# Stores moved to ScalarE's queue, a normalization tied behind the last gate, and norm sums placed between two parts of a product

## The chip, the cores and the metric

The kernel runs on one core of a Trainium2 chip. Five engines work side by side there, each with its own stream of instructions that it takes in order: TensorE (PE, matrix products, with PEld for its weight loads), VectorE (DVE), ScalarE (ACT), GpSimd (POOL) and SyncE (SP), which here only issues DMAs. They wait for one another by semaphores. TensorE writes to PSUM; VectorE and ScalarE read it from there. The metric is the time of one execution on the device, in microseconds.

## What is computed

Three layers follow one another, for a batch of B = 8 sequences of S = 576 tokens, with 8 heads of 64 and so 512 channels:

```python
kv = einsum('bhsd,bhse->bhde', k, v); out = einsum('bhsd,bhde->bhse', q, kv)
x = out / sqrt(mean(out*out, -1) + 1e-6) * g_norm          # per head and token; heads side by side: 512 channels
gate = sigmoid(sum_k conv_w[k] * x shifted by 4-k tokens)   # 5 taps, causal
x = (gate * (x @ w_val)) @ w_out
theta = x @ w_theta
y = w_tok_r @ (x * cos(theta)) + w_tok_i @ (x * sin(theta)) # over tokens
u = x + y;  result = u + relu(u @ w_ch)
```

Activations are 32-bit floats. The weights arrive as 64-bit floats and are decoded on the chip. Each large product is made of three: an operand is split into a rounded part (`h`) and the rest (`l`), and h·h, l·h and h·l are added up.

## The kernel before, in words

Channels lie on the 128 partitions, in four chunks (`m` or `k` = 0 to 3), and tokens along the free dimension, in two halves of 288.

**The first stage** is a loop over the batch, `for i in range(B)` at L392; below, "step i" is one pass of it. A step works on three batch elements at once:

- `value(i)` (L278): for each of four chunks `m`, 24 matmuls make `v` in a PSUM tile of two banks (L274 to L276 in `product`). VectorE multiplies it with the gate (L288, this is what "the gate" means below), ScalarE rounds it to `gh` (L68 in `parts`) and VectorE makes the rest `gl` (L69).
- `first(i)` (L294): the product with w_out, `y`, of four parts; each part runs over four chunks of `gh` and `gl`. Parts 0 and 1 first take chunks 0 to 2 and then chunk 3, since that chunk is finished last. ScalarE copies each finished part to `yo` (L304), two buffers, and SP's queue stores it to DRAM (L305).
- `conv(i + 1)` (L261): for each chunk one ScalarE instruction (L263), four of VectorE in a chain (L265), and the sigmoid (L266). Chunks 0 and 1 are traced at the end of step i, chunks 2 and 3 inside `value(i + 1)`.
- `normalize(i + 1)` (L237): from step 1 on VectorE multiplies `x` with the broadcast reciprocal roots `yb` (L246, two halves), then come `xh` on ScalarE (L68) and `xl` on VectorE (L69). In step 0 the factors come from TensorE instead (L254, L257).
- `attention(i + 2)` (L187), a generator in three pieces: two halves of `o` on TensorE (L200), whose squares (L204) and scaled copies (L205) ScalarE takes out of PSUM; then the norm sums, 64 small matmuls (L212) into one PSUM tile, and the chain of roots on VectorE (L219 to L225). The roots go to DRAM (`rd`, L228) and come back broadcast (`yb`, L233), both by SP's queue.
- `key_value(i + 2)` (L171) on TensorE (L182), and the loads of `kv` and `q` for step i + 3, by SP's queue (L156, L157, L168).

PSUM for all of this is one pool of four tiles of two banks. Each `v`, `y` and `o` tile, the key-value tile and the sums take one of the four and hold it until its reader is done.

**The decoded weights.** `w_theta` (4 pieces, the list `todo`) and the token weights (11 pieces, the list `toks`) are loaded raw (L85), decoded by VectorE and ScalarE (L94 to L98), and the decoded token pieces (`dst_tk`, two buffers) are stored to DRAM (L440) until the second stage loads them. They are traced at a low priority (`LATER`), so that they fill holes, and on VectorE behind the last normalizing instruction of the step (`issue_after(last.ins)`).

**The second stage** (from L444) has the phases, the mix over tokens and the last product; it follows the loop, and its first loads are traced in step 7.

**The order of work.** Python traces the instructions in program order, and a planner puts them into one order per engine: it takes the earliest traced of those that are ready by its own estimate of time, hands out buffers, and adds the semaphores. `issue_after(ins)` is an edge that puts what a block traces on the engine of `ins` behind `ins` in that engine's order; for other engines it says nothing. On the chip the order of each engine stands as planned, also where the real times are others.

Of the kernel before, what the change touches and what calls it, by code (L numbers as in the profile page):

```python
# [34 lines left out]
RATE = (1, 3)  # L35
# [8 lines left out]
def attention_moe_holo_kernel(ctx, tc, kvm, kvt, qt, gn, w_val, conv_w, w_out, w_th, w_tok, w_ch, outT):  # L44
# [5 lines left out]
    nc = tc.nc  # L50
# [8 lines left out]
    def two_banks(name):  # L59

        return pd.tile([P, 2, 512], F32, tag="pd", name=name)[:, :, :HS]
# [4 lines left out]
    def parts(h, l, src):  # L66

        one = nc.scalar.activation(h, src, AF.Copy)  # L68
        return nc.vector.tensor_tensor(l, src, h.bitcast(F32), ALU.subtract), one  # L69
# [18 lines left out]
    def decode(pool, raw, width, name, tag=""):  # L88

        if raw.dtype == F32:  # L90
            return raw
        dst = pool.tile([P, width if tag else DM], F32, tag="dst" + tag if pool is px else "fTt", bufs=(1 if tag else 2) if pool is px else 1, name=f"dst_{name}")[:, :width]
        lo, hi, d = raw[:, :width, 0], raw[:, :width, 1], dst.bitcast(I32)
        nc.vector.tensor_scalar(d, hi, 0x07FFFFFF, 3, ALU.bitwise_and, ALU.logical_shift_left)  # L94
        nc.vector.scalar_tensor_tensor(d, hi, -0x40000000, d, ALU.bitwise_and, ALU.bitwise_or)
        nc.vector.scalar_tensor_tensor(d, lo, 29, d, ALU.logical_shift_right, ALU.bitwise_or)
        nc.scalar.activation(hi.bitcast(F32), hi.bitcast(F32), AF.Square)
        nc.vector.scalar_tensor_tensor(dst, hi.bitcast(F32), TINY, dst, ALU.is_ge, ALU.mult)  # L98
        return dst
# [24 lines left out]
    ydram = [dr.tile([P, NM, S], F32, tag=f"yd{b}", name=f"yd{b}") for b in range(B)]  # L124
# [3 lines left out]
    tokdram = dr.tile([P, 9 * S], F32, tag="td", name="td")  # L128
# [3 lines left out]
    px = px_stack.enter_context(tc.tile_pool(name="px", bufs=1, reuse_waits="tile", side="right"))  # L132
# [104 lines left out]
    def normalize(b, x, y):  # L237


        xh = pa.tile([P, NM, S], F32R, tag="xh", bufs=1, name=f"xh{b}")  # L240
        xl = pa.tile([P, NM, S], F32R, tag="xl", bufs=1, name=f"xl{b}")
        for h in range(2):
            sl = slice(h * HS, (h + 1) * HS)
            v = x[:, :, PAD + h * HS:PAD + (h + 1) * HS]
            if b >= SPREAD:
                last = nc.vector.tensor_tensor(v, v, y[:, :, sl], ALU.mult)  # L246
            else:
                for g in range(2):
                    yb = two_banks(f"yb{b}_{h}_{g}")
                    for t in range(HS // TB):  # L250
                        for j in range(2):
                            k = 2 * g + j
                            rows = slice(32 * k, 32 * (k + 1))
                            nc.tensor.matmul(yb[:, j, t * TB:(t + 1) * TB], sel[rows, h * HS // TB + t, :], y[rows, :],  # L254
                                             start=True, stop=True, tile_position=(32 * k, 0))
                    ch = slice(2 * g, 2 * g + 2)
                    last = nc.vector.tensor_tensor(v[:, ch], yb, v[:, ch], ALU.mult)  # L257
            parts(xh[:, :, sl], xl[:, :, sl], v)
            yield (x, xh, xl), last

    def conv(b, m, x):  # L261
        a = pa.tile([P, S], F32, tag="acc", bufs=4, name=f"acc{b}_{m}")
        nc.scalar.activation(a, x[:, m, 0:S], AF.Copy, scale=cw[:, m * 5:m * 5 + 1])  # L263
        for k in range(1, 5):
            nc.vector.scalar_tensor_tensor(a, x[:, m, k:k + S], cw[:, m * 5 + k:m * 5 + k + 1], a, ALU.mult, ALU.add)  # L265
        nc.scalar.activation(a, a, AF.Sigmoid)  # L266
        return a

    def product(ps, w, m, xh, xl, t0, chunks=range(4)):
        tsl = slice(t0, t0 + HS)  # L270
        wh, wl = w
        for k in chunks:
            ks = slice(k * P, (k + 1) * P)
            nc.tensor.matmul(ps, wh[:, m, ks], xh[:, k, tsl], start=(k == 0), stop=False)  # L274
            nc.tensor.matmul(ps, wl[:, m, ks], xh[:, k, tsl], start=False, stop=False)  # L275
            nc.tensor.matmul(ps, wh[:, m, ks], xl[:, k, tsl], start=False, stop=(k == 3))  # L276

    def value(b, x, xh, xl, sg, between):  # L278
        gh = pa.tile([P, NM, S], F32R, tag="gh", bufs=1, name=f"gh{b}")
        gl = pa.tile([P, NM, S], F32R, tag="gl", bufs=1, name=f"gl{b}")  # L280
        for m in range(NM):
            between(m)
            g = sg[m]
            ps = two_banks(f"v{b}_{m}")
            for h in range(2):
                product(ps[:, h], wv, m, xh, xl, h * HS)
            halves = lambda t: t.rearrange("p (h s) -> p h s", h=2)
            nc.vector.tensor_tensor(halves(g), ps, halves(g), ALU.mult)  # L288
            parts(gh[:, m, :], gl[:, m, :], g)
            if m + EARLY < NM:  # L290
                sg.append(conv(b, m + EARLY, x))
        return gh, gl

    def first(b, gh, gl, between):  # L294
        y = [None] * NM

        def part(m, chunks):
            if y[m] is None:
                y[m] = two_banks(f"y{b}_{m}")
            for h in range(2):  # L300
                product(y[m][:, h], wo, m, gh, gl, h * HS, chunks)
            if 3 in chunks:
                yo = pa.tile([P, S], F32, tag="yo", bufs=2, name=f"yo{b}_{m}")
                nc.scalar.activation(yo.rearrange("p (h s) -> p h s", h=2), y[m], AF.Copy)  # L304
                nc.sync.dma_start(out=ydram[b][:, m, :], in_=yo)  # L305


        part(0, range(3))
        part(1, range(3))
        part(0, (3,))  # L310
        part(1, (3,))
        between()
        part(2, range(4))
        part(3, range(4))

# [46 lines left out]
    raw = {}  # L362
# [29 lines left out]
    for i in range(B):  # L392
        if i == B - 1:
            px_stack.close()
            qx = ctx.enter_context(tc.tile_pool(name="qx", bufs=1, reuse_waits="tile", side="right"))
            ys = load_y(0)
            tls = load_tails(0)
            for k in range(CHFIRST):
                weight_chunk(qx, wch, w_ch, k, "wc")
        two = i + 2 < B  # L400
        if two:
            ahead = attention(i + 2, qs.pop(i + 2))

        def between(m):

            if two and m == 1:
                key_value(i + 2, kvs.pop(i + 2))
                if i + 3 < B:
                    kvs[i + 3] = load_kv(i + 3)
            if two and m == 3:  # L410
                next(ahead)

        gs = value(i, *xs, sg, between)
        if two:
            next(ahead)
            if i + 3 < B:
                qs[i + 3] = load_q(i + 3)
        if i + 1 < B:
            *_, (nxs, last) = normalize(i + 1, *xy)
        if i == 0:  # L420
            for k in range(4):
                weight_chunk(px, wo, w_out, k, "wo", raw=raw[f"o{k}"])
        got = []
        first(i, *gs, lambda: got.append(next(ahead) if two else None))
        xy = got[-1]
        if i + 1 < B:
            xs = nxs
            sg = [conv(i + 1, m, xs[0]) for m in range(EARLY)]
        if 1 <= i < B - 1:
            with tc.high_priority(offset=-LATER), tc.issue_after(last.ins):  # L430
                for _ in range(RATE[0] if i < 6 else 8):
                    if todo:
                        w, src, k, name, scale = todo.pop(0)
                        weight_chunk(px, w, src, k, name, scale)
                for _ in range(RATE[1] if i < 6 else 11):
                    if toks:
                        j = toks.pop(0)
                        sl = slice(j * DM, min((j + 1) * DM, 9 * S))
                        raw = fetch(px, w_tok[:, sl], sl.stop - sl.start, f"tk_{j}")
                        nc.sync.dma_start(out=tokdram[:, sl], in_=decode(px, raw, sl.stop - sl.start, f"tk_{j}"))  # L440

# [7 lines left out]
    last = [None, None]  # L451
# [77 lines left out]
    def halves(b, then=None):  # L529

        nonlocal tls, zt
        f, *y = ys[b]
        if b % 2 == 0:
            zt = phase_tails(b, *tls)
            if then:
                then(8)
        return f, [zt[b % 2]] + phase(b, *y, then)
# [17 lines left out]
    for b in range(B):  # L555
        f, zs = nxt
# [53 lines left out]
```

## Time and profile before

| | us |
|---|---|
| median of 3 runs (lowest, highest) | 753.28 (752.94, 756.45) |
| the profiled execution | 753.31 |
| its span, first to last instruction | 751.5 |
| TensorE busy in the span | 709.7 (94%) |
| VectorE busy | 523.9 (70%) |
| ScalarE busy | 335.9 (45%) |
| mean granted TensorE clock | 0.986 |

Rows of the profile name the engine, the line of the kernel, the operation, and output <- input by the program's names; in a row of the timeline the first two numbers are the start and the length in us, and brackets at the end say how long the engine stood idle before it and what ended that. SPq is SP's DMA queue. Matmuls overlap, so their starts, 0.13 us apart at this size, say more than their lengths.

### The profile page before, as it was taken

Reading aid. Unit: us, or ns where it says so; the run is one execution under the profiler, and the core shown is the slowest. Engines: PE = TensorE matmul, PEld = TensorE weight load, DVE = VectorE, ACT = ScalarE, POOL = GpSimd, SP = SyncE. Lnnn points to the kernel's source line nnn. Section 1 sums busy time; section 2 is a strip of 40 time slices with the busy share of each in tenths; the row PEclk is TensorE's granted clock in tenths of the full one; section 3 lists DMA queues with packets and bytes.
Section 4 is the critical chain, followed back from the end, with each engine's and each line's share of the span. In section 5 each row is a group of like instructions: output and inputs, shape, how many; then the busy total and the mean of one; then the engine's idle time right before and its main releaser. Section 6 shows DMA issues by size and latency. Waiting matters only on the chain.

```text
span 751.5 us, 14674 instructions
## 1 busy us (share of the span) xinstructions
PE 709.7 (94%) x6000; PEld 669.9 (89%) x6000; DVE 523.9 (70%) x930; ACT 335.9 (45%) x560; POOL 20.7 (3%) x72
## 2 busy tenths in 40 slices
PE   1679999999989999889999999999999999999998
PEld 1568999798987999879899899999999998998998
DVE  6389969798879999588983872853853835836504
ACT  2366565637464645376541640621622514514301
POOL 4000000000000000000000000000000000000000
PEclk9779999999999999999999999999999999999999
DMA  9948794979896358534345034163051270160101
GB/s 256 285 140 243 209 229 141 229 228 237 219 238 189 108 136 246 190 102 122 111 138 157 9 119 113 32 174 90 17 164 59 69 179 35 64 175 1 64 1 64
DMA packets 77059, 104.88 MB, mean 140 GB/s; under 512 B 11712, under 2 KB 42560, under 8 KB 76992
## 3 DMA queue, kind: packets, MB, share of 16 engines
q1 hardware_dynamic: 76416, 101.85, 48.5%
q0 software_dynamic: 576, 2.10, 0.9%
q8 instruction: 47, 0.77, 0.4%
q14 instruction: 20, 0.16, 0.1%
HBM read 72.73 MB, written 31.19 MB: 138 GB/s over the span
## 4 chain that ended last, share of the span: by engine, by line
PE 60%; DVE 24%; DMA 8%; ACT 4%; issue 3%; SPq 1%; POOL 0%; DVEq 0%; ACTq 0%; POOLq 0%
PE u L513 10%; PE u L511 10%; PE u L512 10%; DVE acc L265 10%; PE c L276 5%; PE c L274 5%; PE c L275 5%; DMA yb<-rd 4%; PE th L459 3%; PE th L457 3%; PE th L458 3%; DMA kv<-in_kvm_dram 2%; DVE x L246 2%; DVE xl L69 2%; DVE acc L288 2%
## 5 line engine op out<-in xcount | busy, mean ns | idle before, releaser
L516 DVE TENSOR_TENSOR f<-u,f 128x288 f32<-128x288 f32 x64 | 26.5, 455 | 129.8 <-PE u L513 129.8
L265 DVE SCALAR_TENSOR_TENSOR acc<-x,cw,acc 128x576 f32<-128x576 f32 x128 | 100.8, 817 | 1.3 <-ACT acc L263 1.3
L68 ACT ACTIVATE uh<-f 128x288 fp32r<-128x288 f32 x64 | 26.2, 444 | 152.4 <-DVE f L516 152.3
L274 PE MATMUL y<-gh,woh 128*128 128x288 f32 x256 | 77.8, 304 | 7.8 <-DVE acc L288 5.4
L274 PE MATMUL v<-xh,wvh 128*128 128x288 f32 x256 | 77.6, 303 | 0.7 <-DVE acc L288 0.7
L276 PE MATMUL v<-xl,wvh 128*128 128x288 f32 x256 | 76.5, 299 | 0.0
L276 PE MATMUL y<-gl,woh 128*128 128x288 f32 x256 | 75.8, 298 | 0.5 <-DVE gl L69 0.5
L275 PE MATMUL y<-gh,wol 128*128 128x288 f32 x256 | 76.0, 297 | 0.0
L275 PE MATMUL v<-xh,wvl 128*128 128x288 f32 x256 | 76.0, 297 | 0.0
L274 PE MATMUL c<-uh,wch 128*128 128x288 f32 x256 | 75.4, 295 | 0.0
L276 PE MATMUL c<-ul,wch 128*128 128x288 f32 x256 | 75.4, 295 | 0.0
L275 PE MATMUL c<-uh,wcl 128*128 128x288 f32 x256 | 75.4, 294 | 0.0
L274 PEld LDWEIGHTS y<-gh,woh 128*128 128x128 f32 x256 | 48.8, 191 | 11.9 <-DVE acc L288 6.1
L274 PEld LDWEIGHTS v<-xh,wvh 128*128 128x128 f32 x256 | 48.7, 190 | 4.6 <-issue 1.7
L459 PE MATMUL th<-wth,yl 128*128 128x512 f32 x128 | 50.3, 393 | 0.0
L458 PE MATMUL th<-wtl,yh 128*128 128x512 f32 x128 | 50.1, 391 | 0.0
L457 PE MATMUL th<-wth,yh 128*128 128x512 f32 x128 | 50.0, 391 | 0.0
L276 PEld LDWEIGHTS y<-gl,woh 128*128 128x128 f32 x256 | 48.4, 190 | 1.2 <-DVE gl L69 1.2
L276 PEld LDWEIGHTS v<-xl,wvh 128*128 128x128 f32 x256 | 48.6, 190 | 0.3 <-issue 0.2
L275 PEld LDWEIGHTS y<-gh,wol 128*128 128x128 f32 x256 | 48.8, 191 | 0.0
L275 PEld LDWEIGHTS v<-xh,wvl 128*128 128x128 f32 x256 | 48.7, 190 | 0.0
L275 PEld LDWEIGHTS c<-uh,wcl 128*128 128x128 f32 x256 | 48.0, 188 | 0.3
(188 smaller groups left out, 1946.0 us busy)
## 6 DMA issues: line engine op xcount, KB each, us to landing
kv<-in_kvm_dram SPq DMA_DIRECT2D x32, 512.0 KB, 8.6
q<-in_qt_dram SPq DMA_DIRECT2D x32, 288.0 KB, 8.9
yd<-yo SPq DMA_DIRECT2D x32, 288.0 KB, 2.4
f<-yd SPq DMA_DIRECT2D x32, 288.0 KB, 3.7
out_dram<-f SPq DMA_DIRECT2D x64, 144.0 KB, 1.8
sd<-fT SPq DMA_DIRECT2D x64, 128.0 KB, 2.5
yt<-sd SPq DMA_DIRECT2D x8, 1024.0 KB, 5.6
yb<-rd SPq DMA_DIRECT2D x12, 576.0 KB, 8.0
```

What stands on the lines that cost most here:

```text
L68: one = nc.scalar.activation(h, src, AF.Copy)
L265: nc.vector.scalar_tensor_tensor(a, x[:, m, k:k + S], cw[:, m * 5 + k:m * 5 + k + 1], a, ALU.mult, ALU.add)
L274: nc.tensor.matmul(ps, wh[:, m, ks], xh[:, k, tsl], start=(k == 0), stop=False)
L275: nc.tensor.matmul(ps, wl[:, m, ks], xh[:, k, tsl], start=False, stop=False)
L276: nc.tensor.matmul(ps, wh[:, m, ks], xl[:, k, tsl], start=False, stop=(k == 3))
L457: nc.tensor.matmul(ps, yh[:, k, :], wth[0][:, k, :], start=(k == 0), stop=False)
L458: nc.tensor.matmul(ps, yh[:, k, :], wth[1][:, k, :], start=False, stop=False)
L459: nc.tensor.matmul(ps, yl[:, k, :], wth[0][:, k, :], start=False, stop=(k == 3))
L511: nc.tensor.matmul(ps[:, :HS], zh[:, ms], wkh[:, j, sl], start=(i == 0), stop=False)
L512: nc.tensor.matmul(ps[:, :HS], zh[:, ms], wkl[:, j, sl], start=False, stop=False)
L513: nc.tensor.matmul(ps[:, :HS], zl[:, ms], wkh[:, j, sl], start=False, stop=(i == 8))
L516: nc.vector.tensor_tensor(f[:, m, sl], ps[:, :HS], f[:, m, sl], ALU.add)
```

## The change

The diff has five parts:

1. `value` also returns the last `gl` instruction of VectorE, and the loop traces `normalize(i + 1)` under `issue_after` of it: all VectorE instructions of the normalization come behind the last gate's split in VectorE's order. Its ScalarE and TensorE instructions get no edge of their own.
2. The store of each `yo` is issued from ScalarE's queue instead of SP's (32 DMAs of 288 KB).
3. The store of each decoded token piece is issued from ScalarE's queue as well (11 DMAs).
4. In `first` the piece `between()`, which holds the norm sums, the roots and the DMAs of `rd` and `yb`, is traced after chunks 0 to 2 of parts 0 and 1, and no longer after their chunk 3.
5. The special rates for step 6 (8 weight pieces, 11 token pieces) go; the rates are 1 and 3 in every step.

```diff
@@ value
-            parts(gh[:, m, :], gl[:, m, :], g)
+            last, _ = parts(gh[:, m, :], gl[:, m, :], g)
...
-        return gh, gl
+        return gh, gl, last
@@ first
-                nc.sync.dma_start(out=ydram[b][:, m, :], in_=yo)
+                nc.scalar.dma_start(out=ydram[b][:, m, :], in_=yo)
...
         part(0, range(3))
         part(1, range(3))
+        between()
         part(0, (3,))
         part(1, (3,))
-        between()
         part(2, range(4))
         part(3, range(4))
@@ the loop
-            *_, (nxs, last) = normalize(i + 1, *xy)
+            with tc.issue_after(gs[2].ins):
+                *_, (nxs, last) = normalize(i + 1, *xy)
...
-        first(i, *gs, lambda: got.append(next(ahead) if two else None))
+        first(i, *gs[:2], lambda: got.append(next(ahead) if two else None))
...
-                for _ in range(RATE[0] if i < 6 else 8):
+                for _ in range(RATE[0]):
...
-                for _ in range(RATE[1] if i < 6 else 11):
+                for _ in range(RATE[1]):
...
-                        nc.sync.dma_start(out=tokdram[:, sl], in_=decode(px, raw, sl.stop - sl.start, f"tk_{j}"))
+                        nc.scalar.dma_start(out=tokdram[:, sl], in_=decode(px, raw, sl.stop - sl.start, f"tk_{j}"))
```

## The prediction

> **What bounds the kernel now.** I read the page's busy shares first, then TensorE's gaps in order of time, then what VectorE, ScalarE and the DMA queue did in each gap. The page, its first line and its shares:
>
> ```profile
> span 751.5 us, 14674 instructions
> ...
> PE 709.7 (94%) x6000; PEld 669.9 (89%) x6000; DVE 523.9 (70%) x930; ACT 335.9 (45%) x560; POOL 20.7 (3%) x72
> ```
>
> TensorE is busy 94%. The stretches below are steps 1 to 7 of the loop (from the first matmul of `v` to the next step's), the passage to the second stage, and that stage. Columns: stretch and its length, then busy us (instructions) of PE, PEld, DVE, ACT, POOL; granted clock; DMA share; GB/s.
>
> ```profile
> 89.56:121.65 32.09, 32.09 (x370) 30.04 (x369) 25.95 (x44) 18.18 (x28) 1.18 (x5) 1.00 0.73 187
> 121.65:155.88 34.23, 32.71 (x371) 30.12 (x369) 29.61 (x51) 19.48 (x30) 1.19 (x5) 1.00 0.85 220
> 155.88:189.06 33.18, 32.40 (x371) 29.95 (x369) 29.96 (x51) 19.40 (x31) 1.80 (x5) 1.00 0.84 224
> 189.06:224.19 35.13, 32.42 (x371) 30.07 (x370) 27.73 (x49) 17.99 (x29) 1.45 (x5) 1.00 0.89 223
> 224.19:258.91 34.72, 32.71 (x371) 29.97 (x370) 34.37 (x61) 21.39 (x34) 0.39 (x1) 1.00 0.52 159
> 258.91:286.11 27.20, 25.96 (x194) 25.49 (x193) 25.66 (x44) 14.17 (x23) 0.00 (x0) 1.00 0.51 146
> 286.11:315.26 29.15, 27.23 (x194) 27.00 (x193) 22.47 (x33) 10.74 (x17) 1.22 (x2) 0.94 0.68 211
> 315.26:334.00 18.74, 16.30 (x78) 13.14 (x76) 13.83 (x22) 12.32 (x19) 0.00 (x0) 1.00 0.44 130
> 334.00:751.50 417.50, 414.38 (x2853) 398.80 (x2853) 247.67 (x463) 157.10 (x282) 1.06 (x2) 1.00 0.30 89
> ```
>
> Step 1 has no gap in PE: 32.1 us is what a full step costs. Steps 2 to 5 do the same matmuls and take 2.1, 1.1, 3.0 and 2.6 us more (8.9 in all). Steps 6 and 7 have no attention ahead and no norm sums; there DVE (25.66 of 27.20) is nearly full too. From 334 us on the code is not touched, and PE is full. So the change can win at most those 8.9 us and a few of steps 6 and 7.
>
> TensorE's rows beside its gaps (start, length, [idle before <- what ended it]):
>
> ```profile
> 139.91 0.40 PE L274 MATMUL y<-gh,woh 128*128 128x288 f32 x1 [0.25 <-ACT x L205]
> ...
> 142.27 0.29 PE L276 MATMUL y<-gl,woh 128*128 128x288 f32 x1
> 143.55 0.41 PE L274 MATMUL y<-gh,woh 128*128 128x288 f32 x1 [0.99 <-DVE acc L288]
> ...
> 146.76 0.40 PE L276 MATMUL y<-gl,woh 128*128 128x288 f32 x1 [0.28 <-DVE gl L69]
> ...
> 205.65 0.29 PE L276 MATMUL v<-xl,wvh 128*128 128x288 f32 x1
> ...
> 207.27 0.40 PE L274 MATMUL y<-gh,woh 128*128 128x288 f32 x1 [0.20 <-ACT x L205]
> ...
> 209.62 0.29 PE L276 MATMUL y<-gl,woh 128*128 128x288 f32 x1
> ...
> 212.43 0.40 PE L274 MATMUL y<-gh,woh 128*128 128x288 f32 x1 [2.51 <-DVE acc L288]
> ...
> 243.34 0.71 PE L200 MATMUL o<-q,kvs 64*64 64x288 f32 x8 [0.85 <-ACT x L205]
> ...
> 273.57 0.40 PE L274 MATMUL y<-gh,woh 128*128 128x288 f32 x1 [0.98 <-ACT gh L68]
> ...
> 302.51 0.40 PE L274 MATMUL y<-gh,woh 128*128 128x288 f32 x1 [1.92 <-DVE acc L288]
> ```
>
> And VectorE there (steps 2, 4 and 6):
>
> ```profile
> 140.20 2.63 DVE L246 TENSOR_TENSOR x<-x,yb 128x1152 f32<-128x1152 f32 x2 [1.89 <-DMA yb<-rd]
> ...
> 204.91 0.76 DVE L69 TENSOR_TENSOR gl<-acc,gh 128x576 fp32r<-128x576 f32 x1 [0.81 <-ACT gh L68]
> 209.07 2.63 DVE L246 TENSOR_TENSOR x<-x,yb 128x1152 f32<-128x1152 f32 x2 [3.40 <-DMA yb<-rd]
> 211.62 0.75 DVE L288 TENSOR_TENSOR acc<-v,acc 128x576 f32<-128x576 f32 x1
> ...
> 216.58 1.36 DVE L69 TENSOR_TENSOR xl<-x,xh 128x1152 fp32r<-128x1152 f32 x1 [2.27 <-ACT xh L68]
> 217.85 1.54 DVE L265 SCALAR_TENSOR_TENSOR acc<-x,cw,acc 128x576 f32<-128x576 f32 x2
> ...
> 273.25 0.19 DVE L94 TENSOR_SCALAR dst_tk<-raw_tk 128x64 int32<-128x64 int32 x1
> ```
>
> This is the main finding. In step 4 the last matmul of `v` starts at 205.65, so its gate (L288) could run at about 205.95. But VectorE's order has the normalization (L246) ahead of it, and that stands 3.40 us for the broadcast `yb`, starts at 209.07 and takes 2.63 us: the gate runs at 211.62. TensorE meanwhile finishes the first three chunks of `y` part 0 (18 matmuls, to 209.62) and cannot begin part 1: the gate still holds the PSUM tile of the fourth `v`, one of the four in the pool. It goes on at 212.43. Step 2 is the same with 1.89 us of standing.
>
> **The change, part by part.**
>
> *Normalization behind the last gate (VectorE).* The gate then starts when `v` ends, 205.95, and ends at 206.7; part 1 wants its PSUM tile at 209.75. Cover: 3 us. The split that follows (gh 0.69, gl 0.76 and hand-overs) ends about 208.2, the fourth chunk wants it after 212. So three gaps go. By starts, less the usual 0.13 us between matmuls: 143.55 − 142.27 − 0.13 = 1.15; 212.43 − 209.62 − 0.13 = 2.68; and 0.28 at 146.76 as its row has it. Sum: **4.1 us**.
>
> The stall does not vanish, it moves to where it can stand: L246 now waits with `xl` and the convolutions (L265) behind it. In step 4 it starts at 209.07 as before, since the DMA sets it, and nothing but `xl` stands between it and L265: 209.07 + 2.63 + twice 1.3 for `xl` gives a convolution start near 214.3 to 215, against 217.85. In step 2: gl ends about 141.3 instead of L246 starting at 140.20, so L246 is 1.1 us later, and `gl` and gate no longer follow it (1.4 us): even. In steps 1, 3 and 5 the gate stood behind L246 without a gap in PE; there the same exchange wins nothing. Cost: 0, bounds −1 to +1.4 a step, hidden by PE's `y` phase of about 17 us until the next first gate.
>
> *Norm sums between the parts.* The same 64 matmuls, 12 matmuls earlier (1.6 us). Nothing is added on PE. They need all four squares (L204), and one PSUM tile that ScalarE must have emptied. ScalarE in steps 2 and 4:
>
> ```profile
> 145.66 0.65 ACT L204 ACTIVATE sq<-o 128x576 f32<-128x576 f32 x1
> ...
> 206.47 0.75 ACT L205 ACTIVATE x<-o,gsb 128x576 f32<-128x576 f32 x1
> 210.53 1.16 ACT L68 ACTIVATE xh<-x 128x1152 fp32r<-128x1152 f32 x1 [3.31 <-DVE x L246]
> 212.46 0.69 ACT L68 ACTIVATE gh<-acc 128x576 fp32r<-128x576 f32 x1 [0.77 <-DVE acc L288]
> ...
> 214.21 0.65 ACT L204 ACTIVATE sq<-o 128x576 f32<-128x576 f32 x1
> ...
> 216.41 2.78 ACT L263 ACTIVATE acc<-x,cw 128x576 f32<-128x576 f32 x4
> ```
>
> Before, `xh` stood in front of `gh` and of the last two squares and waited 3.31 us for L246. With L246 behind `gl`, `gh` is ready first, and then the squares: 207.3 + 0.7 + 0.65 + 0.73 + 0.65, about 210. PE comes to the sums at 207.27 + 36 × 0.133 = 212.1. So no wait: 0 taken, bounds 0 to 2.8 a step (below). The root chain on VectorE may start some 1.6 to 4.3 us earlier (the 12 matmuls, and the gap), and so do the `rd` store and the `yb` loads on SP's queue, perhaps ahead of the next `kv` loads: a shorter wait at L246, which by now costs nothing.
>
> *Stores by ScalarE's queue.* 32 results of w_out and 11 decoded pieces; the rows are of SP, since ScalarE issues no DMA before:
>
> ```profile
> L305 SPq DMA_DIRECT2D yd<-yo x32: 319/326/683, 82.4 to 316.2; - x32
> ...
> L440 SPq DMA_DIRECT2D td<-dst_tk x11: 319/398/414, 151.1 to 275.1; - x11
> ...
> SPq L305 <- ACT yo L304: 98.5, 25, 12.4
> ...
> SPq L440 <- DVE dst_tk L98: 8.3, 3, 4.0
> ...
> 221.08 0.90 SPq L440 DMA_DIRECT2D td<-dst_tk  x2
> ```
>
> (The first two give min/median/max ns; the next two give us, times, longest.) ScalarE gets 32 × 0.326 + 11 × 0.398 = 14.8 us of issue, about 2 us a step, and has 13 to 18 us idle in each (length less ACT busy above). A `yo` store waits for the copy just before it on the same engine; behind it stand the sigmoids (L266) and convolution starts, whose slack is that idle time: 0. Where a store falls in front of a copy out of PSUM that PE waits for (as 0.85 at 243.34), its 0.4 us counts: from 0 to 11 × 0.4 = 4.4. I take **+0.7**, about two such places, for in most steps PE's wait for L205 is only 0.2.
>
> SP loses 98.5 us of standing for `yo`. Behind it stood the stores of decoded pieces (two at 221.08) and the next raw loads. Freed earlier, the two `dst` buffers let more pieces be decoded in steps 2 to 4, and fewer remain in step 6, where the last one (273.25) runs amid the gates. Bounds: 0 to 0.98 + 1.92 = 2.9, the gaps of steps 6 and 7 that end with late gates. I take **−1.0**: step 7's gap has the second stage's first loads in it as well. Against it, more decoding makes VectorE fuller in steps 2 to 4; that is the first rival's second half.
>
> [...]
>
> *The rates.* The list of weights holds 4 and that of tokens 11; at 1 and 3 a step from step 1 on both are empty after step 4. The special numbers for step 6 found nothing left: no effect.
>
> **Sum.** −4.1 + 0.7 − 1.0 = −4.4. The profiled execution took 753.31 (span 751.5 and 1.8 around it), its median is 753.28: **748.9 us**.
>
> **Rivals.**
>
> *The gain is taken back at the sums or by a fuller VectorE (753.4).* If ScalarE's order stays as it was, the last square ends at 214.86 in step 4 and 146.31 in step 2, and PE, coming at 212.1 and 139.91 + 4.8 = 144.7, stands 2.8 and 1.6 us: 4.4 of the 4.1 won. For: ScalarE is in order. Against: its `xh` now depends on an instruction behind `gl`. The same end has a VectorE that decodes more in steps 2 to 4 and so is late with the middle gates, as in step 5 (34.37 of 34.72 busy, 2.6 us over).
>
> *Slower: ScalarE stands behind the decoded stores (759).* SP waited 8.3 us in 3 cases, 2.8 each, for L98. In ScalarE's queue the same wait holds `gh`, `sq` and `x`, and PE needs the copies out of PSUM. Five steps with one such wait, less the 0.8 that ScalarE stands for a gate anyway (212.46): 5 × 2.0 = 10. 753.3 − 4.1 + 10 = 759. It decides from 0.8 us a step on (4.1 / 5). Against: the pieces are low in the order, and ScalarE has 13 us and more to spare.
>
> *More than that (744.5).* With decoding done by step 5 both tail gaps go (−2.9) and half of what steps 3 and 5 are over (1.9): 753.3 − 4.1 − 2.9 − 1.9 = 744.4.
>
> **How the numbers follow.** Forecast 0.50 (its own range 746.5 to 751), taken back 0.25, slower 0.17, more 0.08. Range **744.5 to 757.5**: it leaves out the lower half of the last case and the upper half of the slower one. A measurement of this kernel can tell about 0.5%, 3.8 us, from no change: faster means under 749.5. Of the forecast 0.43 lies there and 0.07 above; with the last case faster is 0.51, same 0.25 + 0.07 = 0.32, slower 0.17.
>
> **What would show it.** In the changed kernel L246 follows `gl` four in every step, and the PE rows of `y` ended by L288 in steps 2 and 4 (2.51, 0.99) are gone; steps 2 and 4 last about 33 and 32.5 us. Wrong, if L212 shows waits for L204 (first rival), or if ScalarE's idle time is ended by `dst_tk` with L200 or L274 of PE waiting for L205 behind it (second). If L246 still stands for `yb` and the next first `v` or gate then waits for it, the stall has moved onto the path and my cover of 17 us was wrong.

## The result, and the profile after

The changed kernel takes **758.92 us** (median of 12 runs, 755.95 to 761.63); the kernel before took 754.12 beside it (12 runs, 751.04 to 756.64). The ratio is **1.0055, 95% interval 1.0035 to 1.0074**: slower by about half a per cent, where 748.9 and a gain of 0.6% were forecast. The profiled execution took 757.05 us. Two executions far outside the rest, 3125.64 us of e5 (its profiled one) and 994.75 us of the kernel before, stand in no ratio below, and e5's stretches are read from e11, the same kernel.

The stretches of the changed kernel, cut at the same events as before: steps 1 to 7, from first `v` to first `v`, and the passage, from the first `theta` to the first mix. Columns: stretch and its length, then busy us (instructions) of PE, PEld, DVE, ACT, POOL; granted clock; DMA share; GB/s:

```profile
89.20:121.31 32.11, 32.11 (x371) 30.06 (x370) 24.07 (x41) 17.63 (x27) 1.19 (x5) 1.00 0.71 192
121.31:153.41 32.10, 32.10 (x370) 30.05 (x369) 31.01 (x54) 18.98 (x30) 1.23 (x5) 1.00 0.83 233
153.41:191.93 38.52, 35.09 (x371) 31.79 (x370) 30.96 (x54) 21.15 (x33) 1.23 (x5) 0.91 0.75 223
191.93:232.17 40.24, 35.24 (x370) 32.36 (x369) 32.03 (x56) 20.50 (x32) 1.24 (x5) 0.92 0.66 204
232.17:266.56 34.39, 32.49 (x370) 29.97 (x369) 31.40 (x54) 20.51 (x32) 0.12 (x1) 1.00 0.40 118
266.56:293.51 26.95, 25.98 (x194) 25.51 (x193) 24.82 (x40) 12.99 (x20) 0.00 (x0) 1.00 0.68 199
293.51:323.77 30.26, 28.56 (x207) 27.78 (x205) 25.39 (x38) 13.02 (x20) 1.22 (x2) 1.00 0.66 198
323.77:334.75 10.98, 10.98 (x49) 9.02 (x48) 7.76 (x13) 9.34 (x15) 0.00 (x0) 1.00 0.10 29
```

Step 7 and the passage of the kernel before, whose borders in the prediction lay elsewhere:

```profile
286.11:318.02 31.91, 29.99 (x206) 29.26 (x205) 23.70 (x36) 11.91 (x19) 1.22 (x2) 0.95 0.69 215
318.02:330.46 12.44, 11.16 (x50) 8.83 (x48) 9.05 (x15) 9.48 (x15) 0.00 (x0) 1.00 0.31 91
```

Step 2 lost its gaps: 34.23 became 32.10. Step 7 and the passage (323.77 to 334.75) won 1.65 and 1.46; of the 1.65, 1.43 is TensorE's shorter busy time (29.99 to 28.56), as the granted clock of step 7 is 1.00 and was 0.95. But step 3 went from 33.18 to 38.52 (+5.34) and step 4 from 35.13 to 40.24 (+5.11). All other stretches, those ahead of step 1 and behind the passage too, moved by less than 0.6. The 3.8 us between the two spans are these: +10.45 − 2.13 − 1.65 − 1.46, and some −1.4 in small parts.

Against the 32.1 us of a full step, steps 3 and 4 are 6.4 and 8.1 us over. TensorE is idle for 38.52 − 35.09 = 3.4 and 40.24 − 35.24 = 5.0 of it. The rest, 3.0 and 3.1, is longer *busy* time for the same matmuls: the granted clock is 0.91 and 0.92, in steps that ran at 1.00 before. (Against the kernel before, whose steps 3 and 4 had gaps of their own, the loss is the 10.45.)

VectorE in steps 3 and 4 (timeline rows: start, length, instruction, and in brackets the idle time ahead of it and what ended that):

```profile
164.33 0.75 DVE L288 TENSOR_TENSOR acc<-v,acc 128x576 f32<-128x576 f32 x1
...
170.50 0.43 DVE L94 TENSOR_SCALAR dst_tk<-raw_tk 128x512 int32<-128x512 int32 x1 [4.82 <-DMA td<-dst_tk]
170.84 0.75 DVE L69 TENSOR_TENSOR gl<-acc,gh 128x576 fp32r<-128x576 f32 x1
...
172.11 0.75 DVE L288 TENSOR_TENSOR acc<-v,acc 128x576 f32<-128x576 f32 x1
...
179.42 2.62 DVE L246 TENSOR_TENSOR x<-x,yb 128x1152 f32<-128x1152 f32 x2
...
210.15 0.43 DVE L94 TENSOR_SCALAR dst_wt<-raw_wt 128x512 int32<-128x512 int32 x1 [5.53 <-DMA td<-dst_tk]
```

The normalization (L246) now comes behind the last gate, as the change wants it, and stands for nothing. In its place VectorE stands at L94, the first operation of a decode. There are two `dst` buffers, which the token pieces (`dst_tk`) and the pieces of `w_theta` (`dst_wt`) share; the third decode of a step can't start until an earlier store of `td` has landed. That L94 is ordered *between* the second gate (L288 at 164.33) and its `gl`, and the third gate behind it. ScalarE and TensorE wait for those two:

```profile
162.66 0.33 ACTq L441 DMA_DIRECT2D td<-dst_tk  x1
...
172.96 0.68 ACT L68 ACTIVATE gh<-acc 128x576 fp32r<-128x576 f32 x1 [6.62 <-DVE acc L288]
```

```profile
172.92 1.15 PE L200 MATMUL o<-q,kvs 64*64 64x288 f32 x8 [2.63 <-DVE acc L288]
174.87 1.24 PE L200 MATMUL o<-q,kvs 64*64 64x288 f32 x8 [0.80 <-ACT x L205]
...
212.57 0.72 PE L200 MATMUL o<-q,kvs 64*64 64x288 f32 x8 [3.77 <-DVE acc L288]
```

`o` needs a PSUM tile, and the third `v` holds it until its gate has run. The store that step 3 waits for was issued at 162.66, right behind its decode, and had landed by 170.50. Three stretches of the same trace, in the columns of the first fence: the flight of that store, and the two stretches of half clock that go with the gaps:

```profile
162.66:170.50 7.84, 7.63 (x64) 6.62 (x62) 2.95 (x6) 2.00 (x4) 0.00 (x0) 1.00 1.04 286
173.07:179.90 6.83, 6.03 (x32) 4.23 (x29) 4.27 (x7) 5.34 (x10) 0.00 (x0) 0.50 0.70 171
214.03:220.86 6.83, 6.34 (x29) 5.47 (x30) 4.43 (x6) 5.34 (x10) 0.00 (x0) 0.50 0.85 207
```

While it was in flight the DMA engines were full (share 1.04). The DMA issues of 160 to 172 us (queue, count, KB each, median us to landing) name the loads beside it:

```profile
kv<-in_kvm_dram SPq DMA_DIRECT2D x4, 512.0 KB, 10.5
...
td<-dst_tk ACTq DMA_DIRECT2D x1, 256.0 KB, 7.8
```

VectorE's waits in sum (us, times, longest), and the landing of the eleven stores (min/median/max us from issue), after:

```profile
DVE dst_tk L94 <- DMA td<-dst_tk: 7.4, 2, 4.8
DVE dst_wt L94 <- DMA td<-dst_tk: 5.5, 1, 5.5
```

```profile
DMA to landing us min/median/max: 2.5/5.4/8.5
```

and before, where no instruction of VectorE waited for them, and the first store was issued 20 us behind its decode (last operation at 131.0, store at 151.1; after: 134.2 and 134.9):

```profile
DMA to landing us min/median/max: 1.4/2.8/5.8
```

### The profile page after: what moved, and what is told of

It is laid out like the page before. It is cut to its first block, busy times and chain, and to the rows that moved or that the text cites. A ratio compares the mean times of both kernels' runs of the same rounds, so it can differ in the third digit from the quotient of the medians.

```text
span 755.3 us, 14663 instructions
## 1 busy us (share of the span) xinstructions
PE 713.3 (94%) x6000; PEld 672.7 (89%) x6000; DVE 524.2 (69%) x930; ACT 337.6 (45%) x560; POOL 19.5 (3%) x72
## 4 chain that ended last, share of the span: by engine, by line
PE 64%; DVE 22%; ACT 6%; DMA 5%; issue 2%; SPq 0%; ACTq 0%; DVEq 0%
PE u L514 10%; PE u L512 10%; PE u L513 10%; DVE acc L265 9%; PE c L276 4%; PE c L275 4%; PE c L274 4%; PE th L460 3%; PE th L459 3%; PE th L458 3%; DMA td<-dst_tk 3%; DMA kv<-in_kvm_dram 2%; DVE xl L69 2%; DVE acc L288 2%; DVE gl L69 2%
## 5 line engine op out<-in xcount | busy, mean ns | idle before, releaser
L517 DVE TENSOR_TENSOR f<-u,f 128x288 f32<-128x288 f32 x64 | 26.5, 454 | 129.4 <-PE u L514 129.4
```

The costliest lines, as they stand in the source:

```text
L517: nc.vector.tensor_tensor(f[:, m, sl], ps[:, :HS], f[:, m, sl], ALU.add)
```

## The experiments

Every kernel was compared with the kernel before on the same chip. None of them touches the loads and the attention ahead of the first `v`, and still that came between 47.4 and 52.6 us in the profiles; so single profiles are read by their stretches and the totals by the ratios. The two do not add up exactly: from the first `v` on, the stretches' differences to the kernel before are 0.6 to 3.4 us lower than those of the medians (e3: +1.3 and +4.7), which may be because the one profile of the kernel before came there early (48.5). Lengths in us, added up from rows like those above:

| | change | median | ratio, 95% interval | steps 2–5 | steps 6+7 | passage |
|---|---|---|---|---|---|---|
| before | | 752.7 to 754.1 | 1 | 137.3 | 59.1 | 12.4 |
| changed | all | 758.92 | 1.0055 (1.0035–1.0074) | 145.3 | 57.2 | 11.0 |
| e1 | all, td on SP | 745.49 | 0.9896 (0.9879–0.9913) | 129.4 | 61.3 | 11.0 |
| e2 | all, third buffer | 745.81 | 0.9908 (0.9888–0.9927) | 131.0 | 57.3 | 11.0 |
| e8 | both remedies | 746.50 | 0.9913 (0.9881–0.9945) | 130.1 | 57.9 | 11.0 |
| e4 | td alone | 770.53 | 1.0229 (1.0214–1.0244) | 156.2 | 56.6 | 11.0 |
| e6 | yo alone | 751.25 | 0.9979 (0.9953–1.0005) | 135.7 | 58.1 | 11.0 |
| e3 | normalization alone | 757.76 | 1.0064 (1.0046–1.0083) | 130.5 | 55.7 | **24.3** |
| e7 | norm sums alone | 762.03 | 1.0125 (1.0096–1.0155) | 134.3 | 55.6 | **24.9** |
| e10 | normalization, sums | 749.91 | 0.9958 (0.9931–0.9986) | 129.8 | 62.6 | 12.5 |
| e5, e11 | normalization, yo | 754.30 | 1.0015 (0.9995–1.0036) | 129.4 | 55.7 | **21.6** |
| e9 | e3, w_ch ahead of tails | 760.71 | 1.0100 (1.0070–1.0129) | 130.3 | 55.7 | **27.3** |
| e12 | e3, last td on ScalarE | 757.69 | 1.0066 (1.0042–1.0091) | 130.2 | 57.2 | **24.1** |
| e13 | e5, last td on ScalarE | 754.14 | 1.0003 (0.9982–1.0025) | 129.6 | 57.2 | **22.2** |
| e14 | e3, last decode earlier | 747.80 | 0.9931 (0.9904–0.9958) | 130.0 | 59.7 | 12.5 |
| e15 | e5, last decode earlier | 747.17 | 0.9913 (0.9885–0.9942) | 129.4 | 60.0 | 11.0 |

### e1 and e2: two ways to take the buffer wait away

e1, against the changed kernel:

```diff
-                        nc.scalar.dma_start(out=tokdram[:, sl], in_=decode(...))
+                        nc.sync.dma_start(out=tokdram[:, sl], in_=decode(...))
```

> The changed kernel with only the decoded pieces' stores (td) back on SP's queue; results of w_out stay on ScalarE's, norm order and sums stay changed. Three theories. (T) The loss is a wait for a buffer: with the td stores issued right behind the decode, a third decode is ordered between gates of the next step, and VectorE stands at L94 (4.82 and 5.53 us in steps 3 and 4 of the changed kernel) until the td store has landed; TensorE's clock is then halved for 6.83 us. By it steps 3 and 4 go back from 38.5 and 40.2 us to 32 to 34 each, nothing at L94 ends in a wait over 2 us amid the gates, and the time is 758.9 - (38.5 + 40.2 - 2 x 32.6) = about 745 (742 to 750). (R1) ScalarE's own queue stands behind the td stores' waits (my prediction's slower rival): the time falls as well, to about 749, since the same stores leave ScalarE; this run alone doesn't tell R1 from T. (R2) The moved normalization and norm sums cost by themselves: the time stays at 755 to 759.

e2, against the changed kernel (the number of `dst` buffers, L92):

```diff
-... bufs=(1 if tag else 2) if pool is px else 1 ...
+... bufs=(1 if tag else 3) if pool is px else 1 ...
```

> The changed kernel with a third buffer for decoded token pieces (dst of the wide pool: 3 instead of 2); all stores stay on ScalarE's queue. (T) A third decode in a step no longer waits for the landing of an earlier store: the waits at L94 for td (7.4 and 5.5 us in all) fall below 2 us, steps 3 and 4 take 32 to 35 us, the halved clock in them is gone, the time is 743 to 750. (R1) The stores stand in ScalarE's order as before, so ScalarE's stalls stay and the time stays at 756 to 760. (R2) It stays at 755 to 759 too. A middle case: the third buffer only moves the wait to a fourth piece or to the raw loads, then 750 to 755.

Both came down to 745.5 and 745.8; by the ratios, each to the kernel before beside it, that is 1.6% and 1.5%, some 12 and 11 us. Steps 3 and 4 of e1, then of e2 (columns as before):

```profile
154.24:186.35 32.11, 32.11 (x370) 30.06 (x369) 29.57 (x50) 20.14 (x31) 1.24 (x5) 1.00 0.89 252
186.35:219.39 33.04, 32.50 (x370) 29.99 (x369) 30.41 (x54) 18.98 (x29) 1.24 (x5) 1.00 0.82 232
```

```profile
152.66:184.77 32.11, 32.11 (x370) 30.06 (x369) 31.13 (x55) 20.11 (x31) 1.24 (x5) 1.00 0.88 253
184.77:216.99 32.22, 32.18 (x370) 30.06 (x369) 29.09 (x51) 20.28 (x31) 1.23 (x5) 1.00 0.85 243
```

The clock is 1.00 again in both. e1 does it by order. Its VectorE rows in step 3:

```profile
163.36 0.43 DVE L94 TENSOR_SCALAR dst_wt<-raw_wt 128x512 int32<-128x512 int32 x1
...
167.94 0.75 DVE L288 TENSOR_TENSOR acc<-v,acc 128x576 f32<-128x576 f32 x1
168.60 0.42 DVE L94 TENSOR_SCALAR dst_tk<-raw_tk 128x512 int32<-128x512 int32 x1
```

The third L94 stands behind the *third* gate (167.94) and finds its buffer free. It is not that SP's stores land sooner; e1's eleven stores:

```profile
DMA to landing us min/median/max: 2.0/6.8/8.1
```

e2 does it by room: its L94 stays early in the order and waits at most 1.3 us:

```profile
DVE dst_wt L94 <- DMA td<-dst_tk: 1.3, 1, 1.3
```

e2 decides between the theories. It has every store on ScalarE's queue and the moved normalization and sums, and is as fast as e1. So neither ScalarE's issuing (R1) nor the reordering (R2) was what the changed kernel lost by; the third decode's wait for a buffer was.

### e8: both at once

The edits of e1 and e2 together.

> The changed kernel with the td stores back on SP and a third buffer for decoded token pieces: both remedies at once. (T) Each of them alone took away the 4.8 and 5.5 us waits of VectorE in steps 3 and 4 and gave 745.5 and 745.8. If a buffer's release is all that was wrong, both together win nothing more in steps 2 to 4 (32.1 each): 743 to 746, and step 4 at 32.1 to 32.3 instead of the 33.04 of the one with SP's stores. If the third buffer again lets decodes be ordered amid the gates so that VectorE itself is full, steps 3 to 5 rise over 34 and the time is 748 or more.

746.5, just above the 743 to 746 expected: nothing more than either. Steps 2 to 4 are 32.1 each as expected, and step 4's remainder is gone, but step 5 takes 33.8. With the wait gone, one remedy is enough.

### e4 and e6: each kind of store alone on ScalarE's queue

The line of the td store, or that of the yo store, changed from `nc.sync` to `nc.scalar` in the kernel before.

> The kernel before with the td stores alone on ScalarE's queue; results of w_out stay on SP's. (T) The stores issue right behind the decode, more pieces are ordered per step, and VectorE stands for their landing amid the gates in one to three steps, 3 to 5 us each with a halved clock behind: 757 to 763, against 754. (R1) Slower too, but by ScalarE standing for dst_tk ahead of its copies (L205) and splits (L68), with VectorE's waits at L94 under 1 us. (R2) No change: 753 to 755.

> The kernel before with the results of w_out alone stored by ScalarE's queue. If SP's standing for yo (98.5 us of waits) mattered by itself, steps 6, 7 and the passage get shorter by 1 to 3 us while the gaps of steps 2 and 4 (2.13 and 3.0 us) stay: 750 to 753 against 753 to 754. If ScalarE's issues cost (32 x 0.326 us in front of its copies), 754 to 757. If the freed SP fetches earlier and a third decode lands amid the gates, a step takes 36 us or more: 756 to 762.

The yo stores alone make no difference that these runs tell apart (interval 0.9953 to 1.0005), though steps 6, 7 and the passage are 2.4 us shorter in the profile, as expected of SP's standing. Beside the two reorderings they do gain: e1, which is e10 below with the yo stores on ScalarE, is at 0.9896 and e10 at 0.9958, and the intervals lie apart. The td stores alone cost 17 us, above the 757 to 763 expected and more than in the full change, and by the expected mechanism: waits of 6.9 and 6.8 us at L94 for `td` in steps 2 and 4 and one of 7.9 in step 5, whose end the profile doesn't name; those steps take 40 to 43 us. A stretch and a wait of e4:

```profile
124.29:167.21 42.92, 35.65 (x371) 32.28 (x370) 34.67 (x60) 21.02 (x32) 1.19 (x5) 0.88 0.72 203
```

```profile
218.90 0.43 DVE L94 TENSOR_SCALAR dst_tk<-raw_tk 128x512 int32<-128x512 int32 x1 [6.80 <-DMA td<-dst_tk]
```

### e3, e7 and e10: the two reorderings alone, and together

e3 is part 1 of the change alone, e7 part 4 alone. e10 is the changed kernel with both kinds of store back on SP.

> The kernel before with one part of the change alone: the normalization waits behind the last gate's split (gl four). By my prediction's main term the three gaps of steps 2 and 4 go (1.15 + 2.68 + 0.28 = 4.1 us): about 749.5 to 750 against 753.5 to 754 of the kernel before, ratio about 0.9945. (T) says the same, since no store is moved and so no decode is ordered amid the gates by it. (R2), the reorder costs by itself: 755 or more, ratio above 1.002.

> The kernel before with the norm sums alone moved between the parts of y. By my prediction they cost nothing (64 matmuls 1.6 us earlier): 752 to 754.5, ratio within 0.998 and 1.002. Rival (my taken-back case): the last squares are not ready, since ScalarE has xh ahead of them, and TensorE stands 1.6 to 2.8 us at L212 in two or more steps: 756 to 760.

> The changed kernel with both kinds of store back on SP: only the normalization and the norm sums are changed. If T is all (the harm came from the td stores on ScalarE alone), 744 to 748 like e1. If SP's queue matters as in e3 (SP stands for yo, its last td store stands ahead of the loads f and ft, and VectorE then stands at L94 of dst_wc for st), the passage takes 24 us and the time is 753 to 758; the yo stores on ScalarE are then what kept the changed kernel's passage at 11 us.

e3 came out where R2 had it, at 757.8: this reordering alone does cost. But it does not cost at its place: steps 2 to 5 are 6.8 us shorter than before, more than the 4.1 predicted; the loss is in the passage, 24.3 instead of 12.4. e7 is the same picture, at 762.0 above both of its expectations. Together (e10) they have no such loss and gain 0.4%; 749.9 lies between the two cases expected. The passage of e3, in the columns of the stretches, and VectorE in it:

```profile
310.28:334.55 24.27, 11.16 (x50) 8.83 (x48) 12.89 (x21) 11.84 (x19) 0.00 (x0) 0.80 0.56 178
```

```profile
292.31 0.22 DVE L98 SCALAR_TENSOR_TENSOR dst_tk<-raw_tk,dst_tk 128x64 f32<-128x64 f32 x1
...
316.71 0.43 DVE L94 TENSOR_SCALAR dst_wc<-raw_wc 128x512 int32<-128x512 int32 x1 [13.08 <-DMA st<-fTt]
```

VectorE stands 13.08 us for the store `st`; its buffer (tag `fTt`) is shared by the tails' transposes and the decode of w_ch. That store is issued late, at 307.57 instead of 297.83, because everything of the second stage's first rows is late. SP's rows in e3, then in the kernel before:

```profile
292.56 0.32 SPq L441 DMA_DIRECT2D td<-dst_tk  x1
292.93 1.85 SPq L330 DMA_DIRECT2D f<-yd  x4
```

```profile
273.37 2.02 SPq L440 DMA_DIRECT2D td<-dst_tk  x2
275.49 0.85 SPq L330 DMA_DIRECT2D f<-yd  x2
```

The loads `f` go out 17 us later. What holds them is the question of the next runs.

### e5 and e11, e9, e12 and e13: three explanations that fell

e5 and e11 are one kernel, e3 with the yo stores on ScalarE's queue. e9 is e3 with two loops swapped:

```diff
+            for k in range(CHFIRST):
+                weight_chunk(qx, wch, w_ch, k, "wc")
             tls = load_tails(0)
-            for k in range(CHFIRST):
-                weight_chunk(qx, wch, w_ch, k, "wc")
```

e12 and e13 are e3 and e5 with one store moved, that of the last piece:

```diff
-                        nc.sync.dma_start(out=tokdram[:, sl], ...)
+                        (nc.scalar if j == 10 else nc.sync).dma_start(out=tokdram[:, sl], ...)
```

> The kernel before with the normalization behind the last gate and the results of w_out stored by ScalarE's queue; the td stores stay on SP, the norm sums stay behind both parts of y. The normalization alone (e3) won 11 us in the loop and lost 12 at the passage to the second stage, where VectorE stood 13.08 us at L94 of dst_wc for the store st: SP issued the loads f and ft behind a td store at 292.56 us, some 8 us later than the kernel before. Theory P: that loss comes from SP's in-order queue; with the yo stores off it the loads are early again, the passage takes 11 to 13 us instead of 24.3, and the time is 745 to 749. Rival: the loss comes with the normalization's place itself (VectorE's order at the passage); the passage stays at 22 us or more and the time at 755 to 759. Against e1, which has the norm sums between the parts besides: if the sums are worth nothing the two agree within 2 us; if they matter e5 is slower by 3 us or more.

> The same kernel as e5 (normalization behind the last gate, results of w_out stored by ScalarE's queue), for one undisturbed profile. Its median was 754.3, 9 us above e1, which has the norm sums between the parts besides. If the 9 us lie in the passage (24 us with a wait of about 13 us at L94 of dst_wc), it is the order at the passage again and not the sums; if they lie in steps 2 to 5 (waits of TensorE at L212 or of VectorE at L94 for td), the sums' place or the buffer is behind it.

> The kernel before with the normalization behind the last gate (as in e3), and at the passage to the second stage the two pieces of w_ch are decoded ahead of the tails instead of behind them: the same work, the two loops swapped in the program. In e3 the decode shares its one buffer (tag fTt) with the tails' transposes and so VectorE stood 13.08 us at L94 of dst_wc until the store st had landed. Theory P (that wait is e3's whole loss): it is gone, the passage takes 11 to 14 us instead of 24.3, and the time is 743 to 748 (757.8 - 12, to 757.8 - 10 if part comes back). Rival (the passage is late for another reason, SP's late loads f and ft, and would wait elsewhere): the passage stays at 20 us or more and the time at 754 to 758.

> The kernel before with the normalization behind the last gate (e3), and of the eleven td stores the last one alone (the 128x64 piece) issued by ScalarE; the orders of TensorE and VectorE are the same as in e3. In e3 SP issued this store at 292.56 us, when its decode's last operation had run amid the gates of step 7, and the loads f of the second stage's first rows at 292.93 behind it. Theory Q (SP in order: one late store holds the loads, and these set when the passage can begin): f issues at 279 to 285, behind the last yo stores, the 13.1 us wait at L94 of dst_wc falls under 4 us, the passage takes 11 to 15 us instead of 24.3 and the time is 746 to 750. Rival (something else in the norm's new place delays the passage): 755 to 759, the passage at 20 us or more.

> The kernel of e5 and e11 (normalization behind the last gate, yo stores on ScalarE) with the last td store on ScalarE as well; the orders of TensorE and VectorE are the same. In e11 SP stood 21.9 us for this store's decode with f behind it (293.69). Theory Q: f issues at about 272 to 276, the passage takes 11 us instead of 21.6, the time is 742 to 746, the lowest so far. Rival as in e12: 752 to 756.

All three explanations (SP's standing for `yo`, the shared buffer, the last td store ahead of `f`) fell; the passage stayed at 21.6 to 27.3, and e9's time, 760.7, lies above both of its expectations. In e9 the wait only changed its name:

```profile
DVE dst_wc L94 <- DMA raw_wc<-in_w_ch_dram: 12.1, 2, 8.2
```

Without the td store ahead of them in e13, the loads `f` wait just as long, for the decode itself (SP's queue: us in total, times, longest):

```profile
SPq L330 <- DVE dst_tk L98: 23.2, 1, 23.2
```

The pool of the second stage's tiles (`qx`) is opened where that of the raw and decoded pieces (`px`) is closed, and the wait says that `f` isn't loaded until the last piece's last operation (L98, 0.22 us of work) has run. In e3 that is at 292.31, ordered behind the second gate of step 7; in the kernel before it was at 274.81, in step 6.

### e14 and e15: that decode earlier

The last piece is traced without the lowered priority, in the same step as before (LAST is 4); e14 on e3, e15 on e5:

```diff
-                    if toks:
+                    if len(toks) > 1:
...
+            if i == LAST:
+                j = toks.pop(0)
+                sl = slice(j * DM, 9 * S)
+                raw = fetch(px, w_tok[:, sl], ...)
+                nc.sync.dma_start(out=tokdram[:, sl], in_=decode(px, raw, ...))
```

> The kernel of e3 (normalization behind the last gate) with one piece put earlier: the last decoded piece (128x64) without the lowered priority, so that VectorE's order has its four operations among the gates of step 6 and not the last of them amid the gates of step 7. Theory Q is refuted by e12 and e13; their rows show f waiting for dst_tk L98 itself (7.8 and 23.2 us), since f's buffers lie where the pieces' were. Theory S: the late last operation of that decode (292.31 us in e3) holds the loads f and so the passage. By it f issues by 280 us, the wait at L94 of dst_wc for st is gone, the passage takes 11 to 13 us instead of 24.3, and the time is 744 to 749. If the transposes now ordered ahead of step 7's gates hold these up, step 7 takes 31 to 35 us instead of 28.2 and the time is 748 to 753. Rival (something else): passage 20 us or more, 755 to 759.

> The same edit on the kernel of e5, e11 and e13 (normalization behind the last gate, yo stores on ScalarE, td stores on SP). By S: f issues by 278 us, the passage takes 11 us instead of 21.6 to 22.2, step 7 as in the changed kernel 30 us or so, and the time is 742 to 746. Rival: 752 to 756.

The passages came as expected, 12.45 and 10.98, and the times fell: 747.8 against 757.8 for e3, and 747.2 against 754.3 for e5 (742 to 746 was expected of e15; its step 7 takes 32.55 and not some 30). In e14 (timelines of VectorE and of SP's queue, and the passage):

```profile
269.87 0.82 DVE L98 SCALAR_TENSOR_TENSOR dst_tk<-raw_tk,dst_tk 128x64 f32<-128x64 f32 x2
```

```profile
271.13 0.88 SPq L330 DMA_DIRECT2D f<-yd  x2
```

```profile
312.26:324.71 12.45, 11.16 (x50) 8.83 (x48) 9.05 (x15) 9.48 (x15) 0.00 (x0) 1.00 0.31 90
```

The last decode ends at 270.7 instead of 292.5, `f` issues at 271.13, and the passage is 12.45 again. Steps 6 and 7 take 4.0 us more than in e3, which I put down, untested, to the transposes, now ordered ahead of step 7's gates; the net is −10.

## Why the prediction was wrong, step by step

**Normalization behind the last gate, −4.1: right, and too small.** The rows of L246 and of `y` in the changed kernel are as described; step 2 came out at 32.10 (predicted about 33). Measured alone (e3) steps 2 to 5 are shorter by 137.3 − 130.5 = 6.8 us. I had put 0 on steps 3 and 5, but they got shorter by 1.1 and 1.8 as well; step 4 gained 1.7 of the 2.7 expected. The passage gave it all back in e3, through a decode that the new order made late; nothing in the prediction priced that.

**Norm sums, 0: right at their place.** TensorE's waits for the squares, of the kernel before and of the changed one (us in total, times, longest), are the same, and none of them lies between 89 and 260 us, so the first rival's mechanism did not occur:

```profile
PE ss L212 <- ACT sq L204: 4.7, 3, 3.3
```

```profile
PE ss L212 <- ACT sq L204: 4.6, 3, 3.2
```

Steps 2 to 5 of e7 are 3.0 us *shorter* than before, and its loss is the passage, as in e3.

**ScalarE's issues, +0.7: nothing to measure.** e6 with 32 more DMAs on ScalarE is at 0.9979; e2 with all 43 there is as fast as e1 with 32.

**The earlier freed buffers, −1.0: this step failed.** The prediction said: "Freed earlier, the two `dst` buffers let more pieces be decoded in steps 2 to 4, and fewer remain in step 6". Both happened: VectorE's instructions in step 4 went from 49 to 56, in steps 5 and 6 together from 105 to 94, and steps 6, 7 and the passage from 71.6 to 68.2 us, a gain of 3.4. But the prediction set no cost against it other than a fuller VectorE, and took a store's issue for a buffer's release. A store issued right behind its decode, at a DMA share of 1.04, landed 7.84 us later; the order already had the next decode there, amid the gates. So the term that was put at −1.0 cost 10.45 us in steps 3 and 4 against the kernel before. Against a full step they are 6.4 + 8.1 = 14.5 us over, 8.4 in standing and 6.1 in a halved clock. The halved clock was in no term at all. It is the place of the third decode and not the number of pieces: e2 decodes about as many in steps 2 to 4 (160 instructions of VectorE against 164) and loses nothing there.

The DMA share stood at 1.04 while SP's loads and ScalarE's store were in flight together (162.66 to 170.50). The ten 256 KB pieces of the kernel before took 2.8 us to land in the median; here such a store took 7.84 us, and the difference of 5.0 us is about VectorE's wait of 4.82. An estimate from these numbers: a landing after 2.8 us would have come at 165.5, and VectorE reached L94 at 165.7 (170.50 − 4.82).

**The slower rival (759) had the time by chance, not the mechanism.** It had ScalarE standing for L98 in five steps at 2 us each. ScalarE did stand (6.62 us at 172.96), but for a gate, because VectorE stood for the store; it was two steps, at 6.4 and 8.1. The argument against it, that "the pieces are low in the order", was no cover: low priority puts a piece where the planner believes a hole is, and VectorE stood there all the same, 4.82 and 5.53 us at L94 with the next gate ordered behind it, since the buffer wasn't free.

**The rates** were not tried by themselves. By the program both lists are empty after step 4, so the loops of step 6 do nothing at either rate, as the prediction said.

What stays open: why the two reorderings together (e10) leave the last decode early (L98 at 275.24) and each alone makes it late (292.31, 296.49) is a matter of the planner's estimates, and no run here takes it apart.

The fastest kernels are e1, e2 and e8 (e15 with them), whose intervals overlap: the first three are the whole change less the buffer wait, at about 0.99 of the kernel before. Against the changed kernel's 1.0055 that is 1.5%.

## What to carry to other kernels

A queue change is a change of when buffers come free, and here that was set by the landing of a store, 7.84 us behind its issue at 162.66, and not by the issue: look up the landing time in the stretch where it will be issued, and which instruction reuses the buffer, and what stands behind that in its engine's order. Low-priority work was not harmless where what it waited for had no slack (VectorE stood 4.82 and 5.53 us for `td`, with gates ordered behind); one more buffer, or an order that puts it behind the urgent work, bought about 12 us here. Parts of a change to a planned order don't add up (alone: +4.7, +8.7, +17 and −2 us by the medians, together +4.8), so cost the order that comes out, above all the last user of memory that the next stage takes over.

## What the runs showed of the hardware that was not expected

**The clock after a stall.** TensorE ran at half clock (0.50) for 6.83 us in step 3 and again in step 4; that cost 6.1 us beside the 8.4 of standing. In the kernel before a stall of 2.51 us (at 212.43) left it at 1.00, though the one of step 3, with half clock right behind it, is hardly longer, 2.63. In these rows the difference is where the stall falls. The half clock of these two executions begins and ends on a grid of 3.41 us: 179.90 and 214.03 lie 2 and 12 steps of it behind 173.07, and in the kernel before one step of such a grid, 302.98 to 306.39, ran at half clock. Stretches cut on this grid, of the changed kernel, then of the kernel before (28 and 27 steps ahead of that one; columns as above; length less the first busy number is TensorE's idle time):

```profile
169.65:173.07 3.42, 0.79 (x9) 0.56 (x12) 2.57 (x5) 0.11 (x1) 0.00 (x0) 1.00 1.06 316
210.61:214.03 3.42, 0.72 (x8) 0.21 (x8) 3.32 (x6) 2.08 (x4) 0.00 (x0) 1.00 0.66 212
```

```profile
207.41:210.82 3.41, 2.51 (x18) 2.28 (x18) 1.75 (x2) 0.29 (x1) 0.00 (x0) 1.00 1.05 266
210.82:214.23 3.41, 1.80 (x13) 1.81 (x14) 3.41 (x4) 2.64 (x5) 0.00 (x0) 1.00 1.08 233
```

With 2.63 and 2.70 us idle in one such stretch the next one ran at half clock; the 2.51 us fell on two, as 0.90 and 1.61, and the clock stayed. The stall of 0.80 us at 174.87 came when the clock was already halved; the second half-clock stretch follows the one that holds it. In step 4 the first half-clock stretch holds 0.49 us idle and a second follows; the one of the kernel before (302.98 to 306.39) holds none, and the clock is 1.00 behind it. From step 1 to the passage of these two profiles, stretches at a clock of 1.00 with 1.92 us idle and more were followed by half clock (three) and those up to 1.81 were not.

**The landing of a store.** The eleven stores of decoded pieces took from 2.5 to 8.5 us to land in one execution, with a median of 5.4 from ScalarE's queue and 6.8 from SP's (e1); the store of 7.84 us went out in a stretch with 2 MB of `kv` loads and the DMA share at 1.04.
